# Batch 0's first score row regrouped in SBUF, raw weights loaded two ahead and behind the first queries, and part of batch 2 mixed as plain f32

## The chip, the core and the metric

The kernel runs on one core of a Trainium2 chip. The metric is the device time of one execution in microseconds (us). Before the change three runs gave 1308.61, 1309.31 and 1316.12 us; their median, 1309.31 us, is the time before.

## What is computed

Talking-heads attention for 4 batches, 12 heads, 448 positions and head size 64, whose output goes through two feed-forward blocks:

```python
scores = scale * np.matmul(q, k.transpose(0, 1, 3, 2))
scores = np.einsum('bhij,hg->bgij', scores, w_pre)       # mixed over heads
scores = scores - np.max(scores, axis=-1, keepdims=True)
attn = np.exp(scores)
attn = attn / (np.sum(attn, axis=-1, keepdims=True) + 1e-09)
attn = np.einsum('bhij,hg->bgij', attn, w_post)          # mixed again
x = np.matmul(attn, v)                                   # to (1792, 768)
h = (x @ w1) * (x @ w2) @ w3 @ w_out                     # 1024 wide
y = np.maximum(np.maximum(h @ m1, h @ m2), h @ m3) @ o   # 768 wide
```

The weights come as 64-bit floats.

## The kernel before

**Tiles and stages.** Scores are computed for a pair of heads and 112 of the 448 query positions at a time (`scores`, L194): two matmuls per pair, an eviction from PSUM by ScalarE or VectorE, and a store to `sdram[b]`, laid out position by head by key. The mix over heads needs the heads on the partitions. `regroup` (L209) therefore reads `sdram` back into a tile `x` of 120 partitions, 10 positions by 12 heads, with two such groups side by side, 420 KB in all. 45 groups make a batch, so there are 23 steps `(b, p)` of two groups. `mix_softmax` (L228) multiplies each group by a block-diagonal matrix, takes the maximum (L242, VectorE), the exponential (L246, ScalarE) and the scaled second matrix `kwr` (L253, VectorE). `post_mix` (L259) does the second mix with 16 matmuls (L269) and copies the result to the tile `a`. After 6 steps (5 for the last piece) `attend` (L288) multiplies by v, with 96 matmuls, and stores to `xdram`; `load_x` (L308) reads that back, split into a high and a low part.

**f32 and split f32.** A mix of batches 0 and 1 (`b < PLAIN`, with `PLAIN = 2`) is an f32 matmul on `x` itself (L235). From batch 2 on `split_scores` (L217) first makes a high part `xh` (VectorE, L224) and a low part in place (GpSimd, L225), and the mix is three fp32r products per group (L107).

**The weights.** `from_f64` (L87) loads a raw slab of 64-bit weights with a DMA on GpSimd's queue into one of three `wraw` buffers, and converts it with one ScalarE instruction (L93) and four VectorE ones (L94 to L97). There are 64 such loads: 24 of them, w3 in halves and w_out, belong to `fuse` (L321), which multiplies w3 by w_out once and stores the product; there each conversion is followed by ScalarE casts and GpSimd subtractions (L131, L329). The other 40 are used by batch 0's feed-forward part, which also keeps an f32 copy in DRAM for the later batches. In `from_f64` the load stands directly ahead of its conversion in the program.

**The order of the work.** The program first loads batch 0's keys and queries (`load_heads`, L179, on SyncE's queue: pairs 0 and 1, then pairs 2 to 5, then the rest of the queries), computes the first 112 positions of all six pairs into a tile `row` (L435 to L440), which has the only buffer of the tag `a`, and stores `row` to `sdram[0]` in three pieces. Then comes the loop over the 92 steps. In each, `regroup` runs two steps ahead with three `x` buffers, the mix of this step and the second mix of the step before are computed, and matmuls of the feed-forward part, or at first of `fuse`, are put between as fillers at a rate per batch. Scores of the positions still missing (batch 0: one per third of a step, through two buffers `s`) and of the next batch go between as well. A scheduler then orders each engine's instructions; from there on each engine and each DMA queue runs its own list in order. DMAs are issued by SyncE (SP), ScalarE (ACT) and GpSimd (POOL).

Of the kernel before, what the change touches and what calls it, by code (L numbers as in the profile page):

```python
# [7 lines left out]
F32 = mybir.dt.float32  # L8
F32R = mybir.dt.float32r
# [6 lines left out]
B, H, S, D = 4, 12, 448, 64  # L16
# [12 lines left out]
NP = -(-NG // 2)  # L29
CP = CG // 2  # L30
HP = H // 2
PLAIN = 2
F64_MIN = 2.0 ** -15
F64_MAX = 122880.0

# [1 line left out]
def groups(p):  # L37

    n = min(2, NG - 2 * p)
    return n, min(GI, S - 2 * GI * p)  # L40


def chunk(p):
# [6 lines left out]
def attention_talking_heads_moe_kernel(  # L50
# [33 lines left out]
    def banks(tag):  # L84
        return ps.tile([P, 2, 512], F32, tag=tag, name=tag, bufs=1)

    def from_f64(t, src, w):  # L87
        raw = wp.tile([P, PW], I64, tag="wraw", name="wraw", bufs=3)
        nc.gpsimd.dma_start(raw[:, :w], src)
        words = raw[:, :w].bitcast(U32).rearrange("p (x two) -> p x two", two=2)  # L90
        low, high = words[:, :, 0], words[:, :, 1]
        ti = t.bitcast(U32)
        nc.scalar.activation(t, high.bitcast(F32), AF.Abs)  # L93
        nc.vector.tensor_scalar(t, t, F64_MIN, F64_MAX, op0=ALU.max, op1=ALU.min)  # L94
        nc.vector.tensor_scalar(ti, ti, 5, 2, op0=ALU.logical_shift_left, op1=ALU.logical_shift_right)  # L95
        nc.vector.scalar_tensor_tensor(ti, low, 29, ti, op0=ALU.logical_shift_right, op1=ALU.bitwise_or)  # L96
        nc.vector.scalar_tensor_tensor(ti, high, 0xC0000000, ti, op0=ALU.bitwise_and, op1=ALU.bitwise_or)  # L97
# [16 lines left out]

    source = {}
    for names, srcs, n in (
        (("a", "b"), (wa, wb), KH), (("m0", "m1", "m2"), (wm[0], wm[1], wm[2]), KX), (("o",), (wo,), KX),
    ):  # L120
        for m in range(n):
            for name, src in zip(names, srcs):
                kept[name, m] = dram.tile([P, KX * P], F32, name=f"kept_{name}_{m}")
                source[name, m] = src[m]
    stored = set()

    def split_f64(hi, lo, src, w):
        t = wc()[:, :w]
        from_f64(t, src, w)
        nc.scalar.copy(hi, t)  # L130
        nc.gpsimd.tensor_sub(lo, t, hi.bitcast(F32))  # L131

# [5 lines left out]
    def slab(nk, key):  # L138
        hi, lo = slab_tiles()
        hi, lo = hi[:, :nk * P], lo[:, :nk * P]  # L140
        if key in source and key not in stored:
            t = wc()
            from_f64(t, source[key], PW)
            nc.scalar.copy(hi, t)
            nc.scalar.dma_start(kept[key], t)
            stored.add(key)
        else:
            t = lo.bitcast(F32)
            nc.sync.dma_start(t, kept[key])
            nc.scalar.copy(hi, t)  # L150
        nc.vector.tensor_sub(lo, t, hi.bitcast(F32))  # L151
        return hi.rearrange("p (k f) -> p k f", f=P), lo.rearrange("p (k f) -> p k f", f=P)
# [56 lines left out]
    def regroup(b, p):  # L209
        n, m = groups(p)  # L210
        r = m * H
        x = pa.tile([120, 2, S], F32 if b < PLAIN else F32R, tag="x", name="x", bufs=AHEAD + 1)
        src = sdram[b][2 * GI * p:2 * GI * p + n * m].rearrange("(x i) h j -> (i h) x j", x=n)
        nc.sync.dma_start(x[:r, :n] if b < PLAIN else x[:r, :n].bitcast(F32), src)
        xst[b, p] = x

    def split_scores(b, p):  # L217
        if b < PLAIN:
            return
        n, m = groups(p)  # L220
        r = m * H
        x = xst[b, p]
        xh = pa.tile([120, 2, S], F32R, tag="xh", name="xh", bufs=2)
        nc.vector.tensor_copy(xh[:r, :n], x[:r, :n].bitcast(F32))  # L224
        nc.gpsimd.tensor_sub(x[:r, :n], x[:r, :n].bitcast(F32), xh[:r, :n].bitcast(F32))  # L225
        xst[b, p] = (x, xh)

    def mix_softmax(b, p):  # L228
# [2 lines left out]
        pt = banks("m")  # L231
        x = xst.pop((b, p))
        for u in range(n):
            if b < PLAIN:
                nc.tensor.matmul(  # L235
                    pt[:r, u, :S], kp.rearrange("p i h -> p (i h)")[:r, :r], x[:r, u], start=True, stop=True
                )
            else:
                for _ in products(pt[:r, u, :S], [(kp_hi[:r, :r], kp_lo[:r, :r], x[1][:r, u], x[0][:r, u])], 1):
                    pass  # L240
# [80 lines left out]
    def fuse():  # L321
        O = [[big.tile([P, KH, FW], F32R, tag=t, name=t) for t in tags] for tags in (("hhi", "hlo"), ("yhi", "ylo"))]

        def load_out(k):
            t = wc()
            from_f64(t, w_out[k], DM)
            for n, (hi, lo) in enumerate(O):
                nc.scalar.copy(hi[:, k], t[:, n * FW:(n + 1) * FW])  # L328
                nc.gpsimd.tensor_sub(lo[:, k], t[:, n * FW:(n + 1) * FW], hi[:, k].bitcast(F32))  # L329
# [1 line left out]
        def load_w3(m):  # L331
            hi, lo = slab_tiles()
            for x in range(2):
                sl = slice(x * KH * P // 2, (x + 1) * KH * P // 2)
                split_f64(hi[:, sl], lo[:, sl], w3T[m][:, sl], KH * P // 2)
            return [t.rearrange("p (k f) -> p k f", f=P) for t in (hi, lo)]

        w3 = [load_w3(0)]
# [94 lines left out]
    first = load_heads()  # L433
    block_diagonals()
    row = pa.tile([JP, H, S], F32, tag="a", name="row", bufs=1)  # L435
    for pr in range(HP):
        scores(0, pr, 0, first[pr], "mps"[pr % 3], nc.vector if pr % 2 else nc.scalar, row[:, 2 * pr:2 * pr + 2])
        if pr % 2:
            sl = slice(2 * pr - 2, 2 * pr + 2)
            nc.sync.dma_start(sdram[0][:JP, sl], row[:, sl])  # L440
    next(side)

    steps = [(b, p) for b in range(B) for p in range(NP)]
# [106 lines left out]
```

## Time and profile before

| | |
|---|---|
| median of three runs | 1309.31 us |
| the profiled execution, its own time | 1315.45 us |
| its span, first to last instruction | 1313.7 us |
| TensorE matmul busy (PE) | 1249.9 us, 95% |
| VectorE busy (DVE) | 722.4 us, 55% |
| ScalarE busy (ACT) | 615.0 us, 47% |
| GpSimd busy (POOL) | 180.8 us, 14% |
| mean granted TensorE clock | 0.987 of full speed |

How to read the profile: busy time is the time in which an engine had an instruction running, idle time is put down to whatever ended it, and a chain of waits is followed back from the last instruction. L107 is line 107 of the kernel; a tile such as `m<-x,kp` is named by what is written and what is read. Where two instructions of an engine overlap, the time from one start to the next tells more than a duration.

### The profile page before, as it was taken

To read this page: it belongs to the slowest core of one execution; us is meant where nothing else is said; L and a number is where in the kernel's file an instruction comes from. 1 tells how busy PE (TensorE), PEld (TensorE's weight loads), DVE (VectorE), ACT (ScalarE), POOL (GpSimd) and SP (SyncE) were. 2 spreads that over 40 slices of the span, in tenths; PEclk is the share of its full clock that TensorE was granted. 3 is DMA by queue.
4 is the path that set the end of the run, shared out by engine and by line. 5 is a ranking of instruction groups with operands and counts; after the bars stand their busy time and mean duration, and the time that the engine had idled before them with its cause. 6 is when DMAs were issued, how large, how long until landed. Compare 5 with 4: busy or idle time off the path is not lost.

```text
span 1313.7 us, 19457 instructions
## 1 busy us (share of the span) xinstructions
PE 1249.9 (95%) x7650; PEld 1046.3 (80%) x7650; DVE 722.4 (55%) x1036; ACT 615.0 (47%) x1129; POOL 180.8 (14%) x149
## 2 busy tenths in 40 slices
PE   4578999989999999989999999999999999999998
PEld 1245776877877778868888889989999999899998
DVE  5667334448763787985454545565565643344342
ACT  3465555546554554554454444454444443433332
POOL 3333111000000011321111111211121200000000
PEclk9799999989999999989999999999999999999999
DMA  9977768587784687866454544653443324433333
GB/s 286 299 238 240 214 199 288 188 246 266 246 285 134 202 271 215 275 208 191 149 163 141 155 117 136 174 175 110 122 123 112 104 85 133 152 108 120 98 108 114
DMA packets 105970, 236.16 MB, mean 180 GB/s; under 512 B 21972, under 2 KB 61928, under 8 KB 105880
## 3 DMA queue, kind: packets, MB, share of 16 engines
q1 hardware_dynamic: 57400, 125.16, 32.2%
q10 hardware_dynamic: 39168, 63.62, 14.3%
q0 software_dynamic: 9312, 46.16, 11.0%
q8 instruction: 60, 0.98, 0.3%
q14 instruction: 30, 0.25, 0.1%
HBM read 166.48 MB, written 68.42 MB: 179 GB/s over the span
## 4 chain that ended last, share of the span: by engine, by line
PE 80%; DMA 9%; DVE 7%; ACT 2%; issue 2%; POOL 0%; SPq 0%; DVEq 0%; ACTq 0%; POOLq 0%
PE w L107 53%; PE p L269 9%; PE s L296 5%; PE s L200 5%; PE m L235 4%; PE m L107 4%; DMA xdram<-x 2%; DMA xlo<-xdram 2%; DVE wc L96 1%; DMA sdram<-s 1%; DMA wraw<-in_w3T 1%; DVE wc L95 1%; DMA x<-sdram 1%; DVE wc L97 1%; DVE nmax L242 1%
## 5 line engine op out<-in xcount | busy, mean ns | idle before, releaser
L151 DVE TENSOR_TENSOR wlo<-wlo,whi 128x768 fp32r<-128x768 f32 (+1 forms) x144 | 150.2, 1043 | 186.9 <-ACT whi L150 185.0
L150 ACT CAST whi<-wlo 128x768 fp32r<-128x768 f32 (+1 forms) x144 | 125.3, 870 | 270.8 <-DMA wlo<-kept_m 104.2
L107 PE MATMUL w<-yhi,whi 128*128 128x448 f32 (+1 forms) x496 | 190.6, 384 | 2.3 <-ACT z L413 1.2
L107 PE MATMUL w<-yhi,wlo 128*128 128x448 f32 (+1 forms) x496 | 180.1, 363 | 0.0
L107 PE MATMUL w<-ylo,whi 128*128 128x448 f32 (+1 forms) x496 | 179.8, 362 | 0.0
L242 DVE TENSOR_REDUCE nmax<-m 120x2 f32<-120x896 f32 (+1 forms) x92 | 98.3, 1068 | 136.1 <-PE m L235 87.4
L269 PEld LDWEIGHTS p<-kwr,e 120*112 120x112 f32 (+1 forms) x1440 | 160.6, 177 | 13.6 <-issue 3.3
L246 ACT ACTIVATE e<-m,nmax 120x448 f32<-120x448 f32 x180 | 112.6, 630 | 120.5 <-DVE nmax L242 117.4
L269 PE MATMUL p<-kwr,e 120*112 120x120 f32 (+1 forms) x1440 | 164.7, 267 | 2.5 <-DVE kwr L253 1.3
L225 POOL TENSOR_TENSOR x<-x,xh 120x896 fp32r<-120x896 f32 (+1 forms) x46 | 105.7, 2297 | 431.9 <-DVE xh L224 364.1
L107 PE MATMUL w<-hhi,whi 128*128 128x448 f32 (+1 forms) x400 | 154.8, 387 | 5.9 <-ACT hhi L328 4.6
L107 PE MATMUL w<-xhi,whi 128*128 128x448 f32 x384 | 148.5, 387 | 3.6 <-ACT xhi L316 3.6
L107 PE MATMUL w<-hlo,whi 128*128 128x448 f32 (+1 forms) x400 | 146.2, 365 | 1.4 <-POOL hlo L329 0.9
L107 PE MATMUL w<-hhi,wlo 128*128 128x448 f32 (+1 forms) x400 | 145.4, 364 | 0.6 <-DVE wlo L151 0.6
L107 PE MATMUL w<-xlo,whi 128*128 128x448 f32 x384 | 141.9, 370 | 0.0
L107 PE MATMUL w<-xhi,wlo 128*128 128x448 f32 x384 | 141.1, 367 | 0.0
L276 ACT COPY a<-p 112x480 f32<-112x480 f32 (+1 forms) x184 | 92.2, 551 | 65.4 <-PE p L269 56.9
L107 PEld LDWEIGHTS w<-yhi,whi 128*128 128x128 f32 x496 | 93.2, 188 | 26.1 <-issue 16.0
L107 PEld LDWEIGHTS w<-hhi,whi 128*128 128x128 f32 x400 | 75.4, 189 | 32.6 <-issue 14.6
L107 PEld LDWEIGHTS w<-ylo,whi 128*128 128x128 f32 x496 | 93.5, 189 | 8.7 <-issue 2.8
L107 PEld LDWEIGHTS w<-yhi,wlo 128*128 128x128 f32 x496 | 93.3, 188 | 8.7 <-issue 2.0
L107 PEld LDWEIGHTS w<-xhi,whi 128*128 128x128 f32 x384 | 72.7, 190 | 24.5 <-issue 14.1
(83 smaller groups left out, 1766.1 us busy)
## 6 DMA issues: line engine op xcount, KB each, us to landing
x<-sdram SPq DMA_DIRECT2D x88, 420.0 KB, 4.5
sdram<-s ACTq DMA_DIRECT2D x84, 392.0 KB, 4.1
wlo<-kept_m SPq DMA_DIRECT2D x54, 384.0 KB, 3.0
wraw<-in_wm POOLq DMA_DIRECT2D x18, 768.0 KB, 6.8
wlo<-kept_w SPq DMA_DIRECT2D x24, 512.0 KB, 3.6
wlo<-kept_a SPq DMA_DIRECT2D x24, 384.0 KB, 3.0
wlo<-kept_b SPq DMA_DIRECT2D x24, 384.0 KB, 3.2
wraw<-in_w3T POOLq DMA_DIRECT2D x16, 512.0 KB, 6.3
```

Of the source, the lines that this page charges most:

```text
L95: nc.vector.tensor_scalar(ti, ti, 5, 2, op0=ALU.logical_shift_left, op1=ALU.logical_shift_right)
L107: nc.tensor.matmul(out, w, r, start=(k == 0), stop=(k == 3 * n_k - 1))
L150: nc.scalar.copy(hi, t)
L151: nc.vector.tensor_sub(lo, t, hi.bitcast(F32))
L200: nc.tensor.matmul(pt[:JP, o, :S], q[sl, it * JP:(it + 1) * JP], k[sl], start=True, stop=True)
L225: nc.gpsimd.tensor_sub(x[:r, :n], x[:r, :n].bitcast(F32), xh[:r, :n].bitcast(F32))
L235: nc.tensor.matmul(pt[:r, u, :S], kp.rearrange("p i h -> p (i h)")[:r, :r], x[:r, u], start=True, stop=True)
L242: nc.vector.tensor_reduce(out=nmax[:r, :n], in_=pt[:r, :n, :S], axis=AX.X, op=ALU.max, negate=True)
L246: nc.scalar.activation(e[:r, u], pt[:r, u, :S], AF.Exp, bias=nmax[:r, u:u + 1], scale=1.0, accum_out=den[:r, u:u + 1])
L269: nc.tensor.matmul(pt[:, jc // 2, jc % 2, :, u * GI:u * GI + m], e[:r, u, jc * JP:(jc + 1) * JP], kwr[:r, u].rearrange("p (g i) -> p g i", ...
L276: nc.scalar.copy(ast[b][:, 2 * x:2 * x + 2, :, off:off + w].rearrange("p c g i -> p (c g) i"), pt[:, x, :, :, :w].rearrange("p c g i -> p ...
L296: nc.tensor.matmul(pt[o * D:(o + 1) * D, pr // 3, pr % 3, :], vst[b][:, jc, h * D:(h + 1) * D], a[:, jc, h, :], start=(jc == 0), stop=(jc ...
```

## The change

- **Row.** The first 100 of the 112 positions in `row`, that is steps 0 to 4 of batch 0, are regrouped straight from `row` to `x`, by two DMAs for each step from SBUF to SBUF, each from 10 partitions of `row` to 120 partitions of `x` (210 KB). The three stores of `row` become one of its last 12 positions. `row` is therefore read until step 4's `x` has been filled, and the tile `a` of the first second mix, which takes the same buffer, waits for that.
- **Raw weights.** All 64 raw slabs are put into one list in the order of their use. Three are loaded in the prologue: the first behind a one-column GpSimd copy that reads the last pair's queries, the next two behind copies that read what pairs 3 and 5 left in `row`. Later, `next_raw` loads until three are held and then hands one out, so a load stands two conversions ahead of its own.
- **Batch 2.** `PLAIN` becomes `2 * NP + 6` (52), compared with `b * NP + p`: the first six steps of batch 2, 12 groups, are mixed as f32 like batches 0 and 1, with no split.

```diff
-PLAIN = 2
+PLAIN = 2 * NP + 6
+def plain(b, p):
+    return b * NP + p < PLAIN
...
-    def from_f64(t, src, w):
+    sources, raws = [], []
+    for src in [w3T[0], *w_out, *(w3T[m] for m in range(1, KH))]:
+        n = src.shape[1]
+        w = n if n <= PW else n // 2
+        sources += [src[:, x:x + w] for x in range(0, n, w)]
+    sources += [w[m] for m in range(KH) for w in (wa, wb)]
+    sources += [wm[x][m] for m in range(KX) for x in range(3)]
+    sources += [wo[m] for m in range(KX)]
+
+    def load_raw(after=None):
+        src = sources.pop(0)
         raw = wp.tile([P, PW], I64, tag="wraw", name="wraw", bufs=3)
-        nc.gpsimd.dma_start(raw[:, :w], src)
+        if after is not None:
+            nc.gpsimd.tensor_copy(raw.bitcast(F32)[:after.shape[0], :1], after)
+        nc.gpsimd.dma_start(raw[:, :src.shape[1]], src)
+        raws.append(raw)
+
+    def next_raw():
+        while sources and len(raws) < 3:
+            load_raw()
+        return raws.pop(0)
+
+    def from_f64(t, w):
+        raw = next_raw()
...
     def regroup(b, p):
-        src = sdram[b][2 * GI * p:2 * GI * p + n * m].rearrange("(x i) h j -> (i h) x j", x=n)
-        nc.sync.dma_start(x[:r, :n] if b < PLAIN else x[:r, :n].bitcast(F32), src)
+        i0 = 2 * GI * p
+        for u in range(n if b == 0 and i0 + n * m <= JP else 0):
+            nc.sync.dma_start(x[:r, u], row[i0 + u * m:i0 + (u + 1) * m])
+        if b or i0 + n * m > JP:
+            src = sdram[b][i0:i0 + n * m].rearrange("(x i) h j -> (i h) x j", x=n)
+            nc.sync.dma_start(x[:r, :n] if plain(b, p) else x[:r, :n].bitcast(F32), src)
...
+    load_raw(first[HP - 1][1][:, :1])
     for pr in range(HP):
         scores(0, pr, 0, first[pr], "mps"[pr % 3], nc.vector if pr % 2 else nc.scalar, row[:, 2 * pr:2 * pr + 2])
-        if pr % 2:
-            sl = slice(2 * pr - 2, 2 * pr + 2)
-            nc.sync.dma_start(sdram[0][:JP, sl], row[:, sl])
+        if pr % 2 and pr > 1:
+            load_raw(row[:, 2 * pr + 1, :1])
+    last = JP // (2 * GI) * 2 * GI
+    nc.sync.dma_start(sdram[0][last:JP], row[last:])
```

The first place is SP's queue at the start of the program. Before:

```order
L184 DMA qall<-in_qT 128x4x112
L185 DMA qall<-in_qT 128x6x336
L283 DMA v<-in_v 112x4x768
L440 DMA sdram_75<-row 112x1792 x3
L191 DMA k<-in_kT 128x448
L207 DMA sdram_75<-s 112x896
L214 DMA x<-sdram_75 120x2x448 x3
L191 DMA q<-in_qT 128x448
```

The same place in the changed kernel:

```order
L211 DMA qall<-in_qT 128x4x112
L212 DMA qall<-in_qT 128x6x336
L314 DMA v<-in_v 112x4x768
L218 DMA k<-in_kT 128x448
L218 DMA q<-in_qT 128x448
L218 DMA k<-in_kT 128x448
L218 DMA q<-in_qT 128x448
L473 DMA sdram_75<-row 12x5376
L242 DMA x<-row 120x1x448 x6
L234 DMA sdram_75<-s 112x896
L242 DMA x<-row 120x1x448 x4
```

The three stores of `row` and the reads back are gone, the ten DMAs from `row` stand in their place, and four loads of batch 1's keys and queries (224 KB each) have moved ahead of them.

The second place is POOL's queue at the start, behind the small tables `own` and `wide`. Before:

```order
L166 DMA wide<-in_w_post 120x1x12
L89 DMA wraw<-in_w3T 128x512 x2
L89 DMA wraw<-in_w_out 128x768 x2
L131 ISA
L131 TENSOR_TENSOR wlo<-wc,whi 128x512 x2
L329 TENSOR_TENSOR hlo<-wc,hhi 128x384
L329 TENSOR_TENSOR ylo<-wc,yhi 128x384
L89 DMA wraw<-in_w_out 128x768 x2
```

The same place in the changed kernel:

```order
L193 DMA wide<-in_w_post 120x1x12
L105 COPY wraw<-qall 128x1
L106 DMA wraw<-in_w3T 128x512
L105 COPY wraw<-row 112x1
L106 DMA wraw<-in_w3T 128x512
L158 ISA
L158 TENSOR_TENSOR wlo<-wc,whi 128x512
L105 COPY wraw<-row 112x1
L106 DMA wraw<-in_w_out 128x768 x2
L158 TENSOR_TENSOR wlo<-wc,whi 128x512
L106 DMA wraw<-in_w_out 128x768 x2
```

The copies hold the first loads back; the third copy and the first two loads of w_out stand behind the subtraction that needs the first conversion.

The third place is POOL's queue where batch 2's mixes begin (`x<-x,xh` are the splits). Before:

```order
L89 DMA wraw<-in_wm 128x768 x15
L225 TENSOR_TENSOR x<-x,xh 120x896
L89 DMA wraw<-in_wm 128x768 x2
L225 TENSOR_TENSOR x<-x,xh 120x896
L89 DMA wraw<-in_wm 128x768
L89 DMA wraw<-in_wo 128x768 x2
L225 TENSOR_TENSOR x<-x,xh 120x896
L89 DMA wraw<-in_wo 128x768
L225 TENSOR_TENSOR x<-x,xh 120x896
L89 DMA wraw<-in_wo 128x768 x3
L225 TENSOR_TENSOR x<-x,xh 120x896 x18
```

The same place in the changed kernel:

```order
L106 DMA wraw<-in_wm 128x768 x18
L106 DMA wraw<-in_wo 128x768 x6
L256 TENSOR_TENSOR x<-x,xh 120x896 x16
```

All raw loads now stand ahead of the first split, and six splits are gone. On TensorE the list of instructions agrees in kind and order from the first `attend` on, but for the mixes of those six steps.

## Rows read from the trace of the kernel before

**Rows 1.** Busy time by stretch: start:end, length, each engine's busy time, clock, DMA.

```profile
core 0: us, PE busy (x) PEld busy (x) DVE busy (x) ACT busy (x) POOL busy (x), PEclk, DMA share, GB/s
0.00:25.00 25.00, 10.12 (x24) 3.18 (x24) 11.60 (x18) 7.50 (x10) 7.06 (x13) 1.00 0.93 257
25.00:50.00 25.00, 12.20 (x32) 5.10 (x32) 13.20 (x15) 8.92 (x13) 8.15 (x10) 0.69 1.02 343
50.00:126.00 76.00, 59.98 (x280) 34.68 (x280) 58.16 (x90) 43.78 (x88) 26.66 (x30) 0.97 0.79 247
126.00:1314.00 1188.00, 1167.56 (x7318) 1003.32 (x7318) 639.40 (x914) 554.82 (x1019) 138.93 (x96) 0.99 0.55 170
```

**Rows 2.** Timeline of TensorE in the first 126 us: start, length, instruction, idle before.

```profile
14.95 1.84 PE L200 MATMUL s<-kall,qall 64*112 64x448 f32 x4 [6.98 <-DMA qall<-in_qT]
...
81.83 1.67 PE L235 MATMUL m<-x,kp 120*120 120x448 f32 x4
...
125.93 5.14 PE L296 MATMUL s<-a,v 112*64 112x120 f32 x96
```

**Rows 3.** Chain of waits, pieces in order of time: start, length, what.

```profile
3.19 10.30 DMA wraw<-in_w3T
...
27.10 8.16 DMA sdram<-row
35.27 12.18 DMA x<-sdram
47.50 3.36 PE m L235 x4
...
77.28 5.91 DMA sdram<-s
```

**Rows 4.** DMA issues of the first 60 us: size of one, us to landing.

```profile
v<-in_v SPq DMA_DIRECT2D x1, 1344.0 KB, 25.7
wraw<-in_w_out POOLq DMA_DIRECT2D x8, 768.0 KB, 10.9
```

**Rows 5.** Landing of all reads back by L214, from that line's view.

```profile
DMA to landing us min/median/max: 2.3/4.4/17.8
```

**Rows 6.** Timeline of VectorE in the first 126 us.

```profile
25.96 1.08 DVE L202 TENSOR_SCALAR row<-s 112x896 f32<-112x896 f32 x1
...
64.19 2.52 DVE L95 TENSOR_SCALAR wc<-wc 128x768 uint32<-128x768 uint32 x1
...
67.64 0.94 DVE L96 SCALAR_TENSOR_TENSOR wc<-wraw,wc 128x768 uint32<-128x768 uint32 x1
...
69.84 0.55 DVE L95 TENSOR_SCALAR wc<-wc 128x768 uint32<-128x768 uint32 x1
...
98.46 1.09 DVE L202 TENSOR_SCALAR s<-s 112x896 f32<-112x896 f32 x1 [7.84 <-DMA sdram<-s]
```

**Rows 7.** Timeline of TensorE: one f32 mix, and one split mix, among fillers.

```profile
446.71 1.67 PE L235 MATMUL m<-x,kp 120*120 120x448 f32 x4
...
448.42 0.37 PE L107 MATMUL w<-ylo,whi 128*128 128x448 f32 x1
448.63 0.37 PE L107 MATMUL w<-yhi,wlo 128*128 128x448 f32 x1
...
526.82 0.37 PE L107 MATMUL m<-xh,kp_hi 120*120 120x448 f32 x1
...
528.04 0.37 PE L107 MATMUL w<-yhi,whi 128*128 128x448 f32 x1
```

**Rows 8.** Timeline around batch 2's first splits: GpSimd, then VectorE.

```profile
515.18 2.11 POOL L225 TENSOR_TENSOR x<-x,xh 120x896 fp32r<-120x896 f32 x1 [2.17 <-DMA kept_m<-wc]
...
514.41 0.62 DVE L224 CAST xh<-x 120x896 fp32r<-120x896 f32 x1
...
515.37 2.34 DVE L94 TENSOR_SCALAR wc<-wc 128x768 f32<-128x768 f32 x1 [0.26 <-ACT wc L93]
```

**Rows 9.** Timeline at the turn to batch 2: TensorE, ScalarE.

```profile
524.24 0.47 PE L107 MATMUL w<-yhi,whi 128*128 128x448 f32 x1 [1.05 <-DVE den L250]
...
535.09 0.47 PE L107 MATMUL w<-yhi,whi 128*128 128x448 f32 x1 [1.23 <-ACT z L413]
...
540.19 3.86 PE L296 MATMUL s<-a,v 112*64 112x88 f32 x96
...
566.93 1.84 PE L200 MATMUL s<-k,q 64*112 64x448 f32 x4 [6.06 <-ACT s L204]
...
548.65 0.64 ACT L302 COPY x<-s 128x264 f32<-128x264 f32 x2
```

More of the change, by code (lines that the diff above doesn't have):

```diff
@@ L113, in scratch @@
         return tmp.tile([P, S], F32, tag="t", name=name)
-    source = {}
+    source = set()
     for names, srcs, n in (
@@ L123, in attention_talking_heads_moe_kernel, with split_f64 @@
                 kept[name, m] = dram.tile([P, KX * P], F32, name=f"kept_{name}_{m}")
-                source[name, m] = src[m]
+                source.add((name, m))
     stored = set()
-    def split_f64(hi, lo, src, w):
+    def split_f64(hi, lo, w):
         t = wc()[:, :w]
-        from_f64(t, src, w)
+        from_f64(t, w)
         nc.scalar.copy(hi, t)
@@ L142, in slab @@
             t = wc()
-            from_f64(t, source[key], PW)
+            from_f64(t, PW)
             nc.scalar.copy(hi, t)
@@ L211, in regroup @@
         r = m * H
-        x = pa.tile([120, 2, S], F32 if b < PLAIN else F32R, tag="x", name="x", bufs=AHEAD + 1)
-        src = sdram[b][2 * GI * p:2 * GI * p + n * m].rearrange("(x i) h j -> (i h) x j", x=n)
-        nc.sync.dma_start(x[:r, :n] if b < PLAIN else x[:r, :n].bitcast(F32), src)
+        x = pa.tile([120, 2, S], F32 if plain(b, p) else F32R, tag="x", name="x", bufs=AHEAD + 1)
+        i0 = 2 * GI * p
[4 more added lines that the diff above has]
+            nc.sync.dma_start(x[:r, :n] if plain(b, p) else x[:r, :n].bitcast(F32), src)
         xst[b, p] = x
     def split_scores(b, p):
-        if b < PLAIN:
+        if plain(b, p):
             return
@@ L233, in mix_softmax @@
         for u in range(n):
-            if b < PLAIN:
+            if plain(b, p):
                 nc.tensor.matmul(
@@ L325, in load_out @@
             t = wc()
-            from_f64(t, w_out[k], DM)
+            from_f64(t, DM)
             for n, (hi, lo) in enumerate(O):
@@ L334, in load_w3 @@
                 sl = slice(x * KH * P // 2, (x + 1) * KH * P // 2)
-                split_f64(hi[:, sl], lo[:, sl], w3T[m][:, sl], KH * P // 2)
+                split_f64(hi[:, sl], lo[:, sl], KH * P // 2)
             return [t.rearrange("p (k f) -> p k f", f=P) for t in (hi, lo)]
```

## The prediction

> **What bounds the kernel now.** First the busy time by stretch [rows 1]. From 126 us on TensorE is busy 1167.56 of 1188 us: only 20.4 us are idle, so there time is saved by less matmul work or by starting earlier. Before 126 us it is busy 82.3 us (10.12 + 12.20 + 59.98), so 43.7 us are lost. The timeline of TensorE [rows 2] shows what they wait for: queries until 14.95, then the fifth mix at 81.83 and the first `attend` at 125.93. The chain of waits [rows 3] names the rest: the store of `row` (8.16 us), its read back (12.18 us), so that the first mix starts at 47.50. All that time the DMA engines are nearly full (share 0.93 and 1.02) [rows 1]. The second place is the turn to batch 2, where TensorE waits 1.05, 1.23 and 6.06 us [rows 9].
>
> **Queries first.** Pair 2's matmul waits until 14.95 for queries [rows 2], while a raw load, issued at 3.19, takes 10.30 us [rows 3]. With the raw loads held back, SP's first four loads, 448 + 112 + 896 + 224 = 1680 KB, have the DMA engines alone. At the 257 GB/s of the first 25 us [rows 1] that is 6.7 us, and with 2.3 us for issue and landing (the shortest read back, [rows 5]) they are there at 9: 6 us earlier.
>
> **Row complete.** Before, the last copy to `row` ends at 25.96 + 1.08 = 27.0 [rows 6]. Now four pairs follow from 9 us; two matmuls of a pair take 1.84 [rows 2], so about 16. But on VectorE's new list the first conversion stands ahead of the last copy. Its raw load goes out at about 9.5 and takes at most the 10.3 us of rows 3; I take 8. Then 0.7 on ScalarE, 2.0 on VectorE (two thirds of a 768-wide conversion, 0.55 + 0.55 + 0.94 + 0.94 = 3.0, [rows 6]) and 1.1 for the copy: 21.
>
> **From row to x.** Before: 27.10 to 47.50 [rows 3]. Now `x` stands on SP's queue behind 1680 KB, the other queries (1008), v (1344) and four loads of batch 1 (896), 4928 KB or 5.0 MB; with two raw loads 6.1 MB. At 257 GB/s [rows 1] this takes 24 us, so the queue and not `row` decides, at 25. The two DMAs from ten partitions have no row. From below: a read back of the same 420 KB lands in 2.3 us [rows 5]. From above: the store of `row` moved 7 KB per partition in 8.16 us [rows 3]; if the source partition is what limits, 21 KB take 24 us, for each DMA. I take 2.5 us for the pair, as the read back is nearer: the same bytes to the same 120 partitions. First mix at 27.5, 20 us earlier (range 24 to 33, without the upper bound).
>
> [...]
>
> **What is late next.** The conversions. The first w_out loads now go out behind `row`'s last copy, at 21.5, and with about 10 us [rows 4] land at 31; at the first maximum two conversions are done, where the old list had five. From 31 us VectorE is the bound. Up to the fifth mix it has eight 768-wide conversions (24 us) and one of 512 (2), five maxima and two copies at about 1.08 (7.6), and some 3 us of small ones: 36.6. GpSimd's subtractions hold VectorE up: a step of 0.55 took 2.52 [rows 6]. Between 0 and 2 us for each conversion are lost; I take 0.3, as most steps in the old stretch ran beside no subtraction. Fifth mix at 31 + 36.6 + 2.4 = 70, where it was 81.83 [rows 2]: **12 us earlier** (6 to 18). The loads keep this pace if one lands every 5 us, which two ahead with 10 us each just gives.
>
> From there to the first `attend` the lists have the same work, 44.1 us [rows 2]. It is paced by the stores of the two buffers `s` (5.91 us for one [rows 3], VectorE idle for 7.84 [rows 6]), which the change leaves alone. From 126 us on TensorE has no slack to lose the gain in, so it reaches the end.
>
> **Costed at nothing.** The GpSimd copies: it is busy 7.06 of the first 25 us [rows 1]. ScalarE's first copy to `a` waits for step 4's `x`, whose DMAs go out after the second mix, at about 36, and land by 39; the copy's own input is there at about 40. If these DMAs take longer, the exponentials queue behind that copy. "Two ahead" after `fuse`: GpSimd had nothing else to do between the loads, so they already ran as far ahead as three buffers allow.
>
> **Batch 2.** An f32 mix takes 448.42 - 446.71 less one product of 0.21 = 1.50 us, a split one 528.04 - 526.82 = 1.22 [rows 7]: six cost 1.7 us of TensorE. VectorE loses six casts of 0.62 and the wait behind GpSimd, 2.34 where 0.55 is usual [rows 8]: some 14 us in 60. TensorE's waits of 1.05 and 1.23 come from that lateness [rows 9] and should go: 2.3. ScalarE copies `attend`'s result at 548.65, though the matmuls end at 544.05 [rows 9]: 4.6 late, and the 6.06 us wait hangs on this copy's way through DRAM. I credit half, 2.3. Net **2.5 us earlier**; bounds: 1.7 later (no credit) and 5.2 earlier (all).
>
> **Sum.** 12 + 2.5 = 14.5 us. The profiled execution took 1315.45 us, 6.1 above the median of three; off its own time this gives 1301, off the median 1309.31 it gives 1294.8: **1295 us**.
>
> **Rivals.**
> - *The conversions eat the gain.* If each is held up by 1 us and more, or a raw load lands every 7 us, the fifth mix comes at 76 to 80, and 2 to 6 us remain; with 0 to 3 us from batch 2, 1301 to 1309. For it: VectorE starts 31 us in with three conversions more to do. Against it: it idled 25 of the first 50 us [rows 1].
> - *The start gains more.* If no hold-up counts and lighter DMA traffic shortens the stores of `s`, 16 to 22 us: 1284 to 1290. For it: 4 MB through DRAM fewer. Against it: TensorE still needs its 82 us before `attend`, and `s` keeps two buffers.
> - *Slower: ten source partitions are slow.* Ten DMAs follow one another on SP's queue. The fifth mix needs the last of them; it was at 81.83, so from 25 us on each may take 5.7 us. At 10 us each it comes at 125, and all is 43 us later: 1352. At the upper bound of 24 us it would be far worse. For it: the store of `row` at 7 KB per partition in 8.16 us [rows 3]. Against it: that store lay behind v, which took 25.7 us to land [rows 4], so its time says little of a partition. [...]
>
> **Chances and range.** Forecast (1290 to 1300) 0.50, more gain (1284 to 1290) 0.19, eaten (1301 to 1309) 0.22, slower 0.07; 0.02 are left for a case near no change. 1% is 13.1 us, about what a measurement of this kernel can tell from no change, so the line is at 1296.2. Some 0.34 of the forecast lies under it: faster 0.34 + 0.19 = 0.53, within 1% 0.16 + 0.22 + 0.02 = 0.40, slower 0.07. The range 1284 to 1305 holds the forecast, nearly all of the greater gain and half of the eaten one, 0.8.
>
> **What would show it.** Pair 2's matmul at about 9 us; `row` complete near 21; the first mix at 25 to 30 and each DMA from `row` under 4 us; the fifth mix near 70 and the first `attend` near 114; from there equal stretches up to the turn to batch 2. In batch 2's first six steps no GpSimd split, mixes of 1.50 us, TensorE's 1.05 and 1.23 us waits gone and the 6.06 us one shorter. I am wrong if the DMAs from `row` take over 5.7 us each, or if `attend` starts no earlier although the first mix does.

## The result and the profile after

| | before | after |
|---|---|---|
| median of the runs, us | 1310.93 (1308.61 to 1316.12) | 1330.2 (1325.04 to 1331.3) |
| ratio, 95% interval | 1 | 1.0134 (1.0092 to 1.0176) |
| profiled execution, span, us | 1313.7 | 1328.9 |
| first `attend`, us from the span's start | 125.93 | 142.60 |
| from there to the end of the span, us | 1187.8 | 1186.3 |

The changed kernel is **slower by 1.3%**, 19.3 us between the medians. The prediction was 1295 us, and its range ended at 1305. In the two profiles the whole loss lies before the first `attend`: 16.7 us later, then 1.5 us less to the end.

Busy time by stretch after the change, columns as in [rows 1]; the last row is the whole stretch to the first `attend`.

```profile
0.00:25.00 25.00, 8.29 (x24) 3.50 (x24) 4.08 (x10) 4.79 (x6) 3.62 (x11) 0.81 0.91 241
25.00:50.00 25.00, 9.74 (x20) 2.78 (x20) 7.32 (x9) 3.64 (x5) 4.43 (x6) 0.57 0.66 192
50.00:126.00 76.00, 61.17 (x233) 34.61 (x234) 63.39 (x82) 42.05 (x81) 31.62 (x34) 0.82 0.70 215
...
0.00:142.60 142.60, 91.84 (x333) 49.31 (x333) 86.35 (x121) 59.77 (x111) 42.63 (x55) 0.78 0.75 222
```

Against [rows 1], no engine took over: from 25 to 50 us VectorE fell from 13.20 to 7.32 us and the DMA share from 1.02 to 0.66. Everything waited. The same 333 pieces of TensorE before the first `attend` cost 91.84 us where they had cost 82.24, at a mean granted clock of 0.78 of full speed instead of 0.92; from 25 to 50 us it was 0.57, where it had been 0.69 [rows 1]. How much of the loss these 9.6 us make isn't shown.

TensorE's timeline shows what was waited for.

```profile
11.40 1.38 PE L227 MATMUL s<-kall,qall 64*112 64x448 f32 x4 [3.39 <-DMA qall<-in_qT]
...
27.38 1.84 PE L227 MATMUL s<-kall,qall 64*112 64x448 f32 x4 [11.02 <-DVE row L229]
...
42.86 1.84 PE L227 MATMUL s<-kall,qall 64*112 64x448 f32 x4 [7.75 <-ACT s L231]
44.62 2.46 PE L266 MATMUL m<-x,kp 120*120 120x448 f32 x4
51.83 1.84 PE L227 MATMUL s<-kall,qall 64*112 64x448 f32 x4 [4.75 <-ACT s L231]
55.13 3.34 PE L266 MATMUL m<-x,kp 120*120 120x448 f32 x4 [1.46 <-ACT e L277]
...
142.60 5.14 PE L327 MATMUL s<-a,v 112*64 112x120 f32 x96
```

Queries came 3.5 us earlier (14.95 to 11.40). The first mix came at 44.62, only 2.9 us earlier than before [rows 3], and no longer waited for `x` at all: a score stood ahead of it, and that score waited 7.75 us for ScalarE. The kernel before already had this score ahead of its first mix:

```profile
41.42 1.84 PE L200 MATMUL s<-kall,qall 64*112 64x448 f32 x4 [6.07 <-ACT s L204]
47.50 3.34 PE L235 MATMUL m<-x,kp 120*120 120x448 f32 x4 [4.23 <-DMA x<-sdram]
```

So an earlier `x` alone could bring that mix 4.23 us forward, and not 20 (in 2, below, it comes at 43.5). After the change the loss comes behind the first mix: the fifth stands at 95.67, where it was at 81.83. ScalarE's timeline says why:

```profile
29.27 0.92 ACT L231 ACTIVATE s<-s 112x896 f32<-112x896 f32 x1 [1.72 <-PE s L227]
30.22 0.35 ACTq L234 DMA_DIRECT2D sdram<-s  x1
30.61 0.62 ACT L157 CAST whi<-wc 128x512 fp32r<-128x512 f32 x1 [0.43 <-DVE wc L124]
41.89 0.92 ACT L231 ACTIVATE s<-s 112x896 f32<-112x896 f32 x1 [10.65 <-DMA sdram<-s]
42.83 0.31 ACTq L234 DMA_DIRECT2D sdram<-s  x1
50.86 0.92 ACT L231 ACTIVATE s<-s 112x896 f32<-112x896 f32 x1 [8.05 <-DMA sdram<-s]
51.80 0.31 ACTq L234 DMA_DIRECT2D sdram<-s  x1
52.16 1.69 ACT L120 ACTIVATE wc<-wraw 128x768 f32<-128x768 f32 x2 [0.39 <-ACT s L231]
53.75 0.62 ACT L277 ACTIVATE e<-m,nmax 120x448 f32<-120x448 f32 x1
```

Each early score is copied into one of two buffers `s` and stored, two of three by ScalarE and one by VectorE. ScalarE's second copy waits 10.65 us, its third 8.05 us, until an older store has landed. Behind these copies on the same list stand the first step of the w_out conversions and the exponentials of step 0. So the conversions of w_out began at 52, though their first raw loads had gone out at 28.60, and the first had landed 10.5 us later, at 39.1. In the kernel before a conversion stood ahead of the second copy, and its wait for a raw load hid the wait for the store:

```profile
39.68 0.89 ACT L93 ACTIVATE wc<-wraw 128x768 f32<-128x768 f32 x1 [6.65 <-DMA wraw<-in_w_out]
40.47 0.91 ACT L204 ACTIVATE s<-s 112x896 f32<-112x896 f32 x1
```

The other ends of the same knot, VectorE and GpSimd, then SP:

```profile
23.93 0.43 DVE L121 TENSOR_SCALAR wc<-wc 128x512 f32<-128x512 f32 x1 [8.53 <-ACT wc L120]
...
26.25 1.08 DVE L229 TENSOR_SCALAR row<-s 112x896 f32<-112x896 f32 x1
...
47.12 1.09 DVE L273 TENSOR_REDUCE nmax<-m 120x2 f32<-120x896 f32 x1 [13.90 <-PE m L266]
53.09 0.56 DVE L121 TENSOR_SCALAR wc<-wc 128x768 f32<-128x768 f32 x1 [4.88 <-ACT wc L120]
```

```profile
28.60 1.12 POOL L106 DMA_DIRECT2D wraw<-in_w_out  x2
...
57.47 0.53 POOL L106 DMA_DIRECT2D wraw<-in_w_out  x1 [24.38 <-ACT hhi L359]
```

```profile
27.83 14.76 SPq L242 DMA_DIRECT2D x<-row  x6
50.84 0.33 SPq L234 DMA_DIRECT2D sdram<-s  x1
51.28 8.82 SPq L242 DMA_DIRECT2D x<-row  x4
```

GpSimd asked for no raw load between 33 and 57 us, since its three raw buffers stood full behind ScalarE. On SP, 14.76 us pass from the first to the end of the last of six small issues, and by the view of SP's waits 5.6 of them go into a wait for a store of `s` (the rest, 9.2, are the issues themselves):

```profile
SPq L242 <- DMA sdram<-s: 5.6, 1, 5.6
```

That is how the DMA engines came to idle: what frees a buffer for the next transfer stood behind a store. The chain of waits names the same transfers:

```profile
2.25 9.02 DMA qall<-in_qT
...
11.80 11.42 DMA wraw<-in_w3T
...
30.22 11.59 DMA sdram<-s
...
42.83 7.94 DMA sdram<-s
...
59.32 7.50 DMA x<-row
```

### The profile page after: what moved, and what is told of

The parts are those of the page before. It is cut to its first block, busy times and chain, and to the rows that moved or that the text cites. A ratio compares the mean times of both kernels' runs of the same rounds, so it can differ in the third digit from the quotient of the medians.

```text
span 1328.9 us, 19410 instructions
## 1 busy us (share of the span) xinstructions
PE 1260.3 (95%) x7638; PEld 1050.4 (79%) x7638; DVE 710.0 (53%) x1030; ACT 614.7 (46%) x1129; POOL 165.3 (12%) x146
## 3 DMA queue, kind: packets, MB, share of 16 engines
q1 hardware_dynamic: 57065, 123.01, 31.6%
## 4 chain that ended last, share of the span: by engine, by line
PE 81%; DMA 10%; DVE 4%; ACT 3%; issue 2%; SPq 0%; ACTq 0%; DVEq 0%; POOL 0%
PE w L134 53%; PE p L300 9%; PE s L327 5%; PE m L266 5%; PE s L227 5%; PE m L134 3%; DMA sdram<-s 2%; DMA xdram<-x 2%; DMA xlo<-xdram 2%; DMA wraw<-in_w3T 1%; DVE wc L123 1%; ACT s L231 1%; DVE nmax L273 1%; ACT e L277 1%; DMA qall<-in_qT 1%
## 5 line engine op out<-in xcount | busy, mean ns | idle before, releaser
L256 POOL TENSOR_TENSOR x<-x,xh 120x896 fp32r<-120x896 f32 (+1 forms) x40 | 88.6, 2215 | 425.6 <-DVE xh L255 352.9
L231 ACT ACTIVATE s<-s 112x896 f32<-112x896 f32 x84 | 77.1, 918 | 43.6 <-DMA sdram<-s 20.8
```

The costliest lines, as they stand in the source:

```text
L231: nc.scalar.activation(st, pt[:JP, :, :S], AF.Copy, scale=D ** -0.5)
```

## The experiments

Ratios are to the kernel before, timed on the same chip beside each set, with 95% intervals; 1% is 13.1 us. "DMA work" is the DMA share of the stretch to the first `attend` times its length, from each profile (before: 0.86 x 125.9 = 108 us; the rest of the stretch, 18 us, the DMA engines idled). One profile is one execution: the kernel before and the first experiment run the same list up to batch 2, and their first `attend` stands at 125.9 and 120.4. So a first `attend` is read to some 5 us, and the ratios decide.

| | kernel | ratio | first mix | first `attend` | DMA work, idle |
|---|---|---|---|---|---|
| | after | 1.0134 (1.0092 to 1.0176) | 44.6 | 142.6 | 107, 36 |
| 1 | before, batch 2 as f32 | 0.9985 (0.9963 to 1.0007) | 43.7 | 120.4 | 108, 12 |
| 2 | before, x out of row | 1.0071 (1.0049 to 1.0094) | 43.5 | 134.0 | 109, 25 |
| 3 | before, raw loads held, two ahead | 1.0042 (1.0022 to 1.0063) | 42.0 | 128.6 | 107, 22 |
| 4 | after, nothing held | 1.0062 (1.0042 to 1.0081) | 42.1 | 133.7 | 108, 25 |
| 5 | before, four buffers | 0.9983 (0.9969 to 0.9997) | 48.6 | 126.8 | 112, 15 |
| 6 | 2 with four buffers | 1.0008 (0.9987 to 1.0028) | 40.4 | 121.6 | 105, 17 |
| 7 | 4 with four buffers | 1.0032 (1.0010 to 1.0054) | 38.2 | 127.0 | 103, 24 |
| 8 | after, four buffers | 1.0051 (1.0029 to 1.0074) | 37.9 | 124.9 | 104, 21 |
| 9 | 6, three steps out of row | 1.0004 (0.9984 to 1.0023) | 43.2 | 119.7 | 104, 16 |
| 10 | 1 with four buffers | 0.9984 (0.9965 to 1.0003) | 45.2 | 118.9 | 107, 12 |
| 11 | after, first load held alone | 1.0111 (1.0079 to 1.0142) | 42.5 | 136.4 | 106, 30 |
| 12 | 10, three steps out of row | 1.0008 (0.9990 to 1.0025) | 44.5 | 121.3 | 106, 16 |
| 13 | before, v later | 1.0019 (1.0005 to 1.0033) | 41.9 | 121.9 | 106, 16 |
| 14 | 10, v later | 0.9996 (0.9979 to 1.0012) | 43.3 | 121.2 | 103, 18 |
| 15 | before, half of VectorE's steps | 0.9991 (0.9970 to 1.0013) | 49.4 | 120.0 | 107, 13 |
| 16 | after, half of VectorE's steps | 1.0111 (1.0080 to 1.0142) | 42.2 | 138.9 | 110, 29 |
| 17 | before, half the raw bytes | 0.9919 (0.9896 to 0.9941) | 41.6 | 110.4 | 92, 19 |
| 18 | 10, early scores spread | 0.9974 (0.9956 to 0.9991) | 43.8 | 109.9 | 97, 13 |

### The parts one by one: 1 to 4

1, batch 2 as f32 alone (`PLAIN = 2 * NP + 6` and the function `plain`, nothing else of the change).

> The kernel before with one part of the change: batch 2's first six steps are mixed as f32 (PLAIN raised, the rest as before). The changed kernel spent 1186.3 us from the first attend to its end, the kernel before 1187.8, so every theory of the slower start expects the same here: first attend at 126 us as before, the turn to batch 2 shorter by 1 to 2 us, in all 0.998 to 1.000 of the kernel before. My prediction on record gave 2.5 us (0.998). A loss here would mean that the other parts cost less than the comparison of the two traces says.

Measured: 0.9985, 2 us less, with an interval that holds no change. The step's size was about right, and it is too small for these runs to tell.

2, x out of row alone: the change without `load_raw`'s holding copies, with a load issued where it is converted, and `PLAIN = 2 * NP`.

> The kernel before with one part alone: x of the first five steps is regrouped out of row in SBUF, raw weights are loaded as before, batch 2 as before. Theory A, held-back raw loads make the conversions late and that alone costs the time: here the conversions start at 19 us as before, the first mix comes at 30 to 40 instead of 47.5, and the first attend at 115 to 125 instead of 125.9; 1300 to 1310 us. Theory B, the DMAs out of ten partitions are slow and hold up SP's queue and the stores of s behind them: the first attend at 135 to 143 whatever the raw loads do; 1320 to 1330 us.

Measured: 1322.7 us, 9 us over before. Theory A, that held loads alone cost the time, falls, since no raw load is held here. The time is theory B's (the first `attend`, at 134.0, lies just under its 135 to 143), but its mechanism isn't all there is. ScalarE's timeline of this kernel:

```profile
40.78 0.92 ACT L232 ACTIVATE s<-s 112x896 f32<-112x896 f32 x1 [2.79 <-DMA sdram<-s]
...
54.85 0.92 ACT L232 ACTIVATE s<-s 112x896 f32<-112x896 f32 x1 [11.00 <-DMA sdram<-s]
...
74.25 1.02 ACT L308 COPY a<-p 112x480 f32<-112x480 f32 x2 [8.64 <-DMA x<-row]
```

Waits for stores of `s` (11.00) and one for a DMA out of `row`: the copy to `a`, which I had costed at nothing, waits 8.64 us, because `a` takes `row`'s buffer and step 4's two DMAs have to leave it first. The landing of the stores in the first 60 us, from the store line's view, before and in this kernel:

```profile
DMA to landing us min/median/max: 7.0/8.0/10.0
```

```profile
DMA to landing us min/median/max: 11.3/12.9/14.6
```

One store of 392 KB took 12.9 us where it took 8.0. Later, from 150 to 300 us, its median is 4.5 in both. So "which the change leaves alone", as the prediction put it of these stores, is wrong twice: they become the gate, and in 2 they become slower (11.3 us at the least, where 10.0 was the most). After the whole change the two on the chain took 11.59 and 7.94 us.

3, the raw part alone: loads held behind queries and row, two ahead; row through DRAM, batch 2 as before.

> The kernel before with one part alone: raw weights two ahead, the first behind the queries, the next two behind row; row goes through DRAM as before, batch 2 as before. Theory A (late conversions): the first conversion at 23 to 26 us, those of w_out at 45 to 53 instead of 19 to 40, first attend at 135 to 150; 1320 to 1335 us. Theory B (slow DMAs out of row): queries at 11, first mix before 47, first attend at 120 to 130; 1304 to 1314 us.

Measured: 1319.0 us, between the two. The w_out conversions began at 46.7 instead of 21.1 on VectorE, as theory A says, and it cost 5.5 us, less than A's 7 and more. The first `attend`, at 128.6, is not A's (135 to 150) but in theory B's 120 to 130.

4, the changed kernel without the hold:

```diff
-    load_raw(first[HP - 1][1][:, :1])
+    load_raw()
...
-            load_raw(row[:, 2 * pr + 1, :1])
+            load_raw()
```

> The changed kernel, but its first three raw loads wait for nothing (the GpSimd copies that hold them back are left out); row out of SBUF, two ahead and batch 2 stay. Theory A: queries at 13 to 15 us again, conversions from 14 to 19 us on, first attend at 112 to 124; 1298 to 1308 us. Theory B: first attend at 135 to 143 as in the changed kernel; 1320 to 1330 us. If it lies halfway, both count, and the stores of s (11.59 and 7.94 us in the changed kernel) say which.

Measured: 1322.4 us. Holding costs about 9 us of the changed kernel (1.0134 against 1.0062), and the rest costs 8 us over before: both parts lose. "Two ahead" by itself shows no effect: 2 and 1 give 1.0071 - 0.0015 = 1.0056, this kernel has 1.0062.

### Four buffers for the early scores: 5 to 8

```diff
-        st = ... pa.tile([JP, 2, S], F32, tag="s", name="s", bufs=2)
+        st = ... pa.tile([JP, 2, S], F32, tag=buf, name="s", bufs=2)
...
+            ..., buf=("s", "xh")[len(early) % 2])
```

> The kernel before, with four buffers for the 18 early scores of batch 0 instead of two (every second one takes a buffer of the tag xh, which batch 0 does not use). Control for the next three. Theory C, the first steps are gated by the stores of s, whose two buffers make the next score wait for a store: here the wait for x through DRAM hides most of it, so only 1 to 6 us less than the kernel before, 1307 to 1312 where that one takes 1313. Theory B (slow DMAs out of row) has nothing to say here; if this gains over 8 us, the store waits cost the kernel before as much as the changed one.

> Row out of SBUF alone (the second experiment, 1322.7 us, first mix at 43.52, second at 59.35 behind a score that waited 8.73 us for a buffer s), with four buffers for the early scores. Theory C: no score waits for a store in the first 60 us, the first mix by 38, the second by 48, first attend at 112 to 122; 1302 to 1312 us, at or under the control. Theory B: x itself is late, mixes wait for DMA x<-row, first attend after 128; 1318 to 1326 us.

> The changed kernel with its raw loads held back by nothing (the fourth experiment, 1322.4 us), with four buffers for the early scores. Theory C: 1300 to 1310 us, and no slower than the control. Theory B: 1318 to 1326 us as without the buffers.

> The changed kernel (1330.2 us) with four buffers for the early scores and nothing else. Theory A and C together: the stores no longer hold back the exponentials and the conversions' first step on ScalarE, so the conversions of w_out begin at 35 to 42 instead of 53 and the first attend comes at 125 to 135 instead of 142.6; 1312 to 1322 us. If only late raw loads count (A alone): 1326 to 1331 us, as before the edit. If only the stores count (C alone): 1300 to 1310 us, as the run without the hold.

Measured: the buffers give the kernel before 2 us, x out of row 8 us (1.0071 to 1.0008), the kernel without the hold 4 us (1.0062 to 1.0032), the changed kernel 11 us (1.0134 to 1.0051). So far theory C holds: waits for the stores of `s` were the larger part of the changed kernel's loss, and they cost the kernel before little. In 8 the scores ahead of the first mix wait 1.0 to 1.2 us each, the first mix starts at 37.9, and now it does wait for `x`:

```profile
37.87 1.69 PE L266 MATMUL m<-x,kp 120*120 120x448 f32 x2
41.21 1.01 PE L266 MATMUL m<-x,kp 120*120 120x448 f32 x2 [1.65 <-DMA x<-row]
```

In 8 the conversions of w_out begin at 39.60, and what they wait for now is their raw load:

```profile
39.60 1.68 ACT L120 ACTIVATE wc<-wraw 128x768 f32<-128x768 f32 x2 [3.54 <-DMA wraw<-in_w_out]
```

So its 1319.3 us, with the first `attend` at 124.9, is what was expected of A and C together: late raw loads count as well. C alone promised more also in 6 (1302 to 1312 us; 1312.9 measured) and 7 (1300 to 1310; 1315.8): 6 is no faster than the control 5, though its first mix came 8 us earlier. Something behind it bounds the stretch.

### What bounds the stretch then: 9 to 16

9 keeps only three steps out of `row` (`b == 0 and p < 3`, rows 60 to 111 stored), so that no DMA out of `row` waits for a mix; 10 joins the two small gains; 12 adds 9's edit to 10.

> The sixth experiment (row out of SBUF, four buffers for early scores, 1312.86 us beside 1311.86 of the kernel before) with only the first three steps' x out of row; rows 60 to 111 are stored, and steps 3 and 4 read x back as before. The lists of ScalarE, VectorE and TensorE keep their order. Theory D: row and a share one buffer, so ScalarE's first copy to a waits for the last DMA out of row, which goes out only behind the second mix (7.16 us to land in the sixth experiment, the copy done at 67): here all DMAs out of row go out at once at 27, the copy waits for none, and the first attend comes 2 to 6 us earlier; 1306 to 1311 us. Theory E, VectorE's conversions bound the stretch whatever ScalarE's copy does: the same as the sixth experiment, 1311 to 1315 us.

> The kernel before with batch 2's first six steps as f32 and four buffers for the early scores; row through DRAM and raw loads as before. The two parts measured 0.9985 and 0.9983 apart; if they add, 0.997, 1308 us. If the four buffers only move the wait to the conversions (theory E) and the f32 steps gain in batch 2 alone, they still add, since the places are 400 us apart. Either alone: 0.998 to 0.999.

> All that gained, with the part of the change that was worth keeping if theory D holds: three steps of x out of row, four buffers for the early scores, batch 2's first six steps as f32, raw loads as in the kernel before. Theory D: 2 to 6 us under the run with the buffers and f32 alone, 1302 to 1307 us (0.993 to 0.997). Theory E: no better than that run, 1306 to 1312 us (0.996 to 1.000).

Measured: 1312.3, 1309.9 and 1313.0 us. Theory D's wait was real (7.16 us on the chain of 6) and its removal was worth nothing (1.0004 against 1.0008). x out of `row` gains in none of its forms; in 12 it costs 3 us against 10, at intervals that overlap. The two small gains of 10 didn't visibly add.

11, only the first raw load held:

```diff
-            load_raw(row[:, 2 * pr + 1, :1])
+            load_raw()
```

> The changed kernel, in which only the first raw load waits for the queries; the two behind row are held by nothing, and go out behind the first on GpSimd's queue at about 12 us. Changed kernel 1.0134, without any hold 1.0062 of before. Theory A1, what costs is that the first w_out loads wait for row (28 us): here 1.005 to 1.008, 1318 to 1322 us, and the conversions of w_out begin by 40 instead of 53. Theory A2, what costs is that the first load waits for the queries (12 us instead of 3), so all loads behind it move 8 us: 1.011 to 1.015, 1326 to 1331 us.

Measured: 1.0111, theory A2. Holding the very first load costs about 6 us (against 4); holding the next two, about 3 more, at overlapping intervals.

13 holds v and batch 1's first pairs behind a maximum (`nc.vector.tensor_copy(t[:JP, 0, :1], newest[-1][:JP, :1])` ahead of the DMA), 14 is the same on 10. 15 and 16 return from `from_f64` ahead of its last two VectorE steps for w_out and w3.

> The kernel before, with v of batch 0 (1344 KB) and the first two pairs of batch 1 (896 KB) loaded behind the maxima of steps 2, 4 and 6 instead of in the first 14 us; nothing else. Theory F, the DMA engines bound the start: 2.24 MB fewer in the first 50 us, at the 257 to 343 GB/s measured there 6.5 to 8.7 us, so the w_out loads land earlier by about that, the first mix at 38 to 42 and the first attend 5 to 9 us earlier; 1303 to 1308 us, 0.993 to 0.997. Theory E, VectorE's conversions bound it: x earlier, but the first attend unchanged within 2 us; 1310 to 1314 us.

> The same late loads, with batch 2's first six steps as f32 and four buffers for the early scores (these two alone 0.9984). Theory F: 0.990 to 0.995, 1300 to 1306 us. Theory E: 0.997 to 1.000, 1308 to 1312 us.

> The kernel before, but in the conversions of w_out and w3 VectorE leaves out its last two steps of four (the low word and the sign are not put in, so the fused weights are others); ScalarE, GpSimd, DMAs and TensorE keep their work. A conversion of 768 columns takes VectorE about 1.1 us instead of 3.0. Theory E: before the first attend some 12 conversions of 1.2 to 1.9 us each are saved, the first attend at 108 to 118; 1298 to 1306 us. Theory F: w_out still lands when it lands, the first attend within 4 us of before; 1307 to 1313 us.

> The changed kernel with the same two VectorE steps left out of the conversions of w_out and w3. Theory E, VectorE's late start is what the held loads cost: first attend at 118 to 128 instead of 142.6; 1305 to 1316 us, at or near the kernel before with the same cut plus at most 8 us. Theory F, it is the loads themselves: first attend after 132; 1318 to 1328 us, over 10 us above the kernel before with the same cut.

Measured: 1.0019 and 0.9996: 2.24 MB out of the first 50 us gain nothing (theory F falls as put). 0.9991 and 1.0111: half of VectorE's early work is worth 1 us to the kernel before and 3 us to the changed kernel, whose stretch now reads

```profile
0.00:138.90 138.90, 88.16 (x332) 49.36 (x332) 49.80 (x84) 59.23 (x111) 42.84 (x56) 0.80 0.79 232
```

VectorE is busy 49.80 us instead of 86.35, and `attend` still comes at 138.9. Theory E falls as put: VectorE's work alone bounds neither kernel. The numbers of 16 are those of its theory F, by which the held loads themselves cost the time. But a second wait has come up in the place of VectorE's, ScalarE's for the stores of `s` up to the first `attend`. In the changed kernel, then in 16:

```profile
ACT s L231 <- DMA sdram<-s: 20.2, 3, 10.7
ACT s L235 <- DMA sdram<-s: 26.2, 4, 11.0
```

In 15 these waits are 12.8 us, and 2.4 in the kernel before. So 15 and 16 leave the two buffers as a gate, and don't tell what VectorE would be worth without it; no run has four buffers and the shorter conversions.

### The amount of DMA work: 17 and 18

What was left is in the table's last column: in 1 to 16 the DMA engines work 103 to 112 us before the first `attend`, whatever is moved about, and kernels differ by how long they idle. Work and idle time add up to the stretch by definition, so this says where the time went and not yet why. 13 couldn't gain by this, since v has to be there for the first `attend` anyway.

```diff
+        h = w // 2 if half[0] else w
-        nc.gpsimd.dma_start(raw[:, :w], src)
+        nc.gpsimd.dma_start(raw[:, :h], src[:, :h])
```

```diff
-        if early:
+        if early and (len(early) > 12 or p > 2 and third == 0 or p > 8 and third == 1):
```

> The kernel before, but each raw load of w_out and w3 brings half of its columns, and the conversion uses them twice (the fused weights are others; all engines keep their work, the lists shift by a few places). Theory G, the amount of DMA work bounds the stretch to the first attend: some 6.5 of 33.7 MB fewer, at 268 GB/s 24 us; TensorE's own 82 us and the 15 us to the queries then bound it, first attend at 100 to 110 where it is 120 to 126; 1290 to 1300 us. Theory H, it is a chain of waits between engines, in which a transfer's size counts little: first attend at 115 to 124; 1306 to 1313 us.

> Batch 2's first six steps as f32 and four buffers for the early scores (0.9984 together), and the 18 early scores spread: six in the first two steps as before, then one per step up to step 8, the rest in steps 9 to 11, each still two steps before it is read. Seven of them with their stores, 2.7 MB, go behind the first attend. Theory G: 10 us less DMA work before it, the first attend at 108 to 114; TensorE has 7 us of these matmuls to do later, so 2 to 4 us are gained: 0.995 to 0.997, 1305 to 1309 us. Theory H: no store waits to save beyond those that the buffers took away, 0.998 to 1.001, 1309 to 1313 us.

```profile
0.00:110.42 110.42, 80.14 (x333) 42.73 (x333) 76.66 (x122) 59.62 (x111) 45.16 (x53) 0.89 0.83 251
```

```profile
0.00:109.89 109.89, 78.15 (x320) 43.95 (x321) 75.61 (x109) 56.17 (x105) 39.47 (x50) 0.94 0.88 269
```

Measured: 17 takes 10.6 us off (0.9919) with DMA work of 92 instead of 108; first `attend` at 110.4. That is the only edit in the study that made the kernel before faster by more than 3.5 us, and no engine lost an instruction by it (VectorE's busy time fell from 83 to 77 us all the same). Theory G predicted a little more (24 us of DMA work, the first `attend` at 100 to 110, 1290 to 1300 us; 1302.2 measured), theory H less; 16 us less DMA work gave about two thirds of itself. 17 doesn't separate the amount of work from the time of a single load. Its raw loads also landed sooner (in the first 110 us those of w_out took 7.8 us at the median, where it was 10.9, and those of w3 4.6, where it was 6.1), and in the kernel before ScalarE waits 30.6 us for such loads, each of which needs a buffer that a conversion has to free. A chain of loads and conversions would be shorter here too. 18 puts stores and scores behind the first `attend`, which comes at 109.9, as G said, with less for the engines to do before it (TensorE 78.15 us, 83.76 in 10); but TensorE makes up those scores later, and 0.9974 (0.9956 to 0.9991) is left, just short of G's 0.995 to 0.997: 3.4 us faster than before, the fastest kernel here that leaves nothing out. Against 10 its intervals overlap.

## Why the prediction was wrong

- **Queries.** Predicted 9, came 11.40: the mechanism held. The chain's transfer took 9.02 us, just my 6.7 and 2.3; but it was issued only at 2.25, which I left out.
- **Row complete.** Predicted 21, came 26.25 + 1.08 = 27.3, no earlier than before. Mis-sized term: the first raw load, held to 11.80, took 11.42 us, not 8, above even the 10.3 I named as the most. I saw that the first conversion stands ahead of `row`'s last copy on VectorE; that ate the earlier queries whole.
- **From row to x: the failed step.** I let the first mix follow `x`, at 27.5, and counted the stores of the two buffers `s` only from the fifth mix on. The first mix came at 44.62, behind early scores on TensorE's list whose copies wait for those buffers. Before, ScalarE's wait for a raw load and TensorE's for `x` hid the store waits. I had read the store at 5.91 us from a place at 77 us; in the first 60 us it took 7.0 to 10.0 before, and 11.59 on the chain after. Run 8 shows the size: four buffers alone bring the first mix to 37.9 and return 11 us.
- **What is late next: the same step in the sum.** The term of 12 us let the conversions begin when their loads land, at 31, and put the fifth mix at 70. VectorE began them at 53.09 and the fifth mix came at 95.67, 26 us late. Of the 22 us at the start, 8 are the loads, which went out at 28.60 instead of 21.5 and landed at 39.1; in the rest ScalarE was held by the stores, until 52. From there to the fifth mix it took 42.6 us where I had 39, so that stretch was sized about right; whether VectorE sets it is open, since 16 took half of VectorE's steps away and gained 3 us.
- **Costed at nothing.** The copy to `a` waited for step 4's DMAs: 8.64 us in 2, and 0.17 in the changed kernel, where ScalarE had just waited 3.50 us for a raw load. "Two ahead" was worth nothing, as predicted.
- **Ten source partitions.** The rival that ends slower had the right sign, but not the mechanism. It let the fifth mix wait for the last of the ten DMAs; that one landed at 66.82, and the fifth mix came at 95.67. My own sign was wrong, too: each DMA was to take under 4 us, and the last one took 7.50 us on the chain after, 9.66 in 2 and 7.16 in 6, above the 5.7 that I had named. After the change the last two were issued at 58.50 and 59.32, and the pair took 8.3 us (58.50 to 66.82). With four buffers and no wait behind a mix (9) they no longer cost anything measurable (1.0004). They weren't slow enough to decide by themselves; in 2 the stores of `s` took 12.9 us at the median, where it had been 8.0, and SP needed 9.17 us to issue six. My estimate of 2.5 us for a pair was 5.8 too low for that last one, which ran beside a raw load (issued at 57.47, waited for by ScalarE until 65.80).
- **The stretch of 44.1 us from the fifth mix** became 46.9 (95.67 to 142.60): equal within a few us.
- **Batch 2.** Predicted 2.5 earlier; 2 in run 1, not told apart from nothing. The waits of 1.05 and 1.23 us [rows 9] are gone from the stretch of 490 to 545 us, and the one of 6.06 is now 4.78:

```profile
579.27 1.84 PE L227 MATMUL s<-k,q 64*112 64x448 f32 x4 [4.78 <-ACT s L231]
```

The base of the error is one: [rows 1] showed the DMA engines at 0.93 and 1.02 while `x` was waited for. I read that as a reason to take bytes out, and then priced transfers from quiet places. The resource that was full was also one on which the start depends, and the change let it idle: held raw loads (9 us by 4) and copies that stand behind stores (11 us by 8) overlap in this, and without both (7) 1.0032 is left. Where the idle time fell: from 25 to 50 us the share went from 1.02 to 0.66, 9 us of DMA time; over the whole stretch idle went from 18 to 36 us, and the first `attend` came 16.7 us later.

**Open.** Why x out of `row` gains nothing even in 9 and 12 isn't settled. It moves 2 MB less before the first `attend` (31.6 MB after, 33.75 before), but the DMA work is 107 us where it was 108; in 9 it is 3 to 4 us less than in 1 and 10, and the idle time 4 us more. Nor is it settled whether the amount of DMA work or the landing of single raw loads made 17 faster, or whether the slower stores of 2 come from the DMAs out of `row` or from raw loads that then run beside them. A DMA out of ten partitions on idle DMA engines wasn't timed alone.

## What to carry to other kernels

When a wait is removed, look in the in-order list for what stands between it and the next of its kind: here the stores of early scores, with two buffers, had been hidden behind waits for raw loads and for `x`. Where the DMA engines are nearly full until a point that everything waits for, sum the DMA work up to there and ask of each edit whether it lets them idle; here, holding raw loads back behind the queries and `row` cost 9 us (4). Price a transfer from the stretch in which it will run, not from the shortest one in the trace: the store of `s`, priced here at 5.91 us, took 11.59 on the chain after.

## What the runs showed of the hardware

- A store of 392 KB took 8.0 us at the median in the first 60 us of the kernel before and 4.5 from 150 to 300 us. In the first 60 us of 2 it took 12.9; there SP issued six DMAs out of `row` from 26.65 to 35.82 us, and GpSimd five raw loads of 768 KB from 27.66 to 49.72. No run here isolates what made the stores longer.
- DMAs from SBUF to SBUF out of ten partitions held SP longer at their issue than reads from DRAM: in 2 six took 9.17 us, 1.0 of it a wait, so 1.4 us each, where three of the kernel before took 1.68 us, 0.56 each. A pair of them later took 1.64 us in 2, 0.82 each, where single reads took 0.32 and 0.35. The issue of an ordinary load of k behind v took 6.72 us in 2, so the pattern isn't all that makes an issue long.
- Taking half of VectorE's steps away from every early conversion, 36 us of its busy time in the changed kernel, moved that kernel by about 3 us (1.0134 to 1.0111, at intervals that overlap), while ScalarE's waits for the stores of `s` rose from 20.2 to 26.2 us.
